# A spectral transform and MLP on one core: MLP chunks of 512 tokens instead of 470

## The chip, the cores and the metric

The kernel runs on one core of one Trainium2 chip. The metric is device time in microseconds of one execution. Before the change three runs gave 2720.18, 2721.32 and 2723.31 us, a median of 2721.32 us.

TensorE (PE) multiplies matrices into the eight PSUM banks; VectorE (DVE), ScalarE (ACT) and GpSimd (POOL) do the elementwise work; SyncE (SP) issues most of the DMAs and ACT some. Each engine runs its instructions in the order in which they were put on its queue.

## The reference

Two stages. First a filter in the frequency domain on x of shape (8, 3008, 256): a real FFT along the sequence, a complex projection of the 256 channels, a soft threshold, and the inverse FFT. Then an MLP on the 24064 tokens that result, with d_model 256 and d_ff 2048.

```python
X = np.fft.rfft(x, axis=1)
Yr = Xr @ w_r - Xi @ w_i + b_r
Yi = Xr @ w_i + Xi @ w_r + b_i
Yr = np.sign(Yr) * np.maximum(np.abs(Yr) - 0.01, 0.0)      # Yi alike
y = np.fft.irfft(Yr + 1j * Yi, n=3008, axis=1)
h = y.reshape(24064, 256) @ w_in
out = np.maximum(0.01 * h, h) @ w_out
```

## The kernel before

The FFT of length 3008 = 47 x 64 is one transform over n1 (47 values, taken as 24 sums and differences) and one over n2 (64 values). The 64 values of n2 are written as 13 g + s, with five g and thirteen s; s = 12 has only four g that carry data. The stages for one batch are these generators and functions.

- `fwd(b)` (line 169): loads x in seven pieces (`load`), makes sums and differences (`fold`), multiplies by the matrices `fa` (`stage_a`) and stores to `u_dram`.
- `mid(b)` (line 231): for twelve pairs of k1, loads from `u_dram`, transforms over n2 (`stage_b`), projects and thresholds (`proj`), transforms back over k2 (`stage_g`) and stores to `v_dram`.
- `v_load(ci)` and `inverse(ci, eh)` (lines 349, 362): load one (batch, s) pair of sets, that is two neighbours in the list of all (batch, s), and make its tokens: four matmuls for each of the two halves of the channels, then on ACT a copy `odd`, on DVE a sum and a difference into `y`, and the split of `y` into `yh` and `yl`. `odd` and `y` have one buffer each.
- `moe_h(ci, f)` and `moe_o(ci, f)` (lines 389, 407): one of 16 blocks of 128 of the hidden dimension of one chunk of tokens. `moe_h` runs six matmuls into a `psh` bank (two banks), applies leaky relu and splits the result into `gh` and `gl`. `moe_o` runs six matmuls that add to the two `pso` banks of the chunk.

Most operands are held as two parts (`hi` and `lo`, of type float32r), and a product is three matmuls, hi x hi, hi x lo and lo x hi (`products`, line 70). Plain float32 products, used in the prologue and for the two 128-wide transforms, appear as two instructions in the profile.

Tokens come in chunks: one chunk is one pair of sets, 10 x 47 = 470 tokens, or 9 x 47 = 423 where the pair has an s = 12 (matmuls then take 424 columns). There are 44 chunks of 470 and 8 of 423. `moe()` (line 431) goes over chunks and blocks; `moe_o` follows `moe_h` by LAG = 3 steps; at block 4 it loads the next chunk's pair, at blocks 10 and 12 it runs the inverse for it.

The order of the work around it: a prologue does `fwd` of batches 0 to 2, `mid(0)`, and the conversion of the MLP's weights from float64 (`load_mlp`). Then `v_load(0)` and both halves of `inverse(0)` stand ahead of the first `moe_h`. During the MLP of batch b the streams `mid(b + 1)` and `fwd(b + 3)` are put between its steps; the position goes from b to b + 1, and each stream is complete at 0.75 of it. The program is put on the queues by a scheduler that moves instructions ahead where it finds them ready, so the trace doesn't follow the source order to the letter.

Buffers that the change touches: `yh` and `yl` have two each, and two of batch 0's x pieces (`XT`, line 167) and the weights `w_r` and `w_d` (line 97) use the same ones in the prologue.

Of the kernel before, what the change touches and what calls it, by code (L numbers as in the profile page):

```python
# [8 lines left out]
F32 = mybir.dt.float32  # L9
# [15 lines left out]
# High words of float64 numbers, read as float32: the last that float32 holds, and the one that becomes zero.  # L25
# [5 lines left out]
def spectral_mlp_kernel(  # L31
# [38 lines left out]
    def products(dst, pairs):  # L70
        """dst = sum of lhsT.T @ rhs over pairs of operands, each float32 or two parts of it."""
        terms = []
        for l, r in pairs:
            terms += [(l[0], r[0]), (l[0], r[1]), (l[1], r[0])] if len(l) == 2 else [(l[0], r[0])]
        for i, (a, b) in enumerate(terms):
            nc.tensor.matmul(dst, a, b, start=(i == 0), stop=(i == len(terms) - 1))  # L76
# [62 lines left out]
    def load_mlp():  # L139
        """Piece by piece; the last ones stay off the buffers that the MLP needs."""  # L140
# [26 lines left out]
    XT = [(("xa", 3), ("xb", 3))] * 3 + [(("yh", 2), ("gh", LAG + 1)), (("yl", 2), ("gh", LAG + 1))] * 2  # L167
# [63 lines left out]
    def mid(b):  # L231
# [17 lines left out]
        def stage_b(j):  # L249
            """Xr, s Xi and their sum for two k1, with the sign s of the half spectrum."""  # L250
# [26 lines left out]
        def proj(j):  # L277
            """With K = (Xr + Xi) w_r: Yr = K - Xi (w_r + w_i) + b_r, Yi = K + Xr (w_i - w_r) + b_i."""
# [63 lines left out]

# [6 lines left out]
    def v_load(ci):  # L349
        vin = sb.tile([PA, 2, 2, D], F32, name="vin", tag="vin")  # L350
        (b, s, _), (b1, _, _) = chunks[ci]
        for c in range(2):
# [4 lines left out]
            for i, (b_, s_, _) in enumerate(chunks[ci]):  # L357
                vv = v_dram[b_].rearrange("c k (g s) d -> c (k g) s d", g=NG)
                sync.dma_start(vin[:, c, i, :], vv[c, :, s_, :])
        v_t[ci] = vin  # L360

    def inverse(ci, eh):
        """The even and the odd part of the tokens in n1, of which n1 is the sum and 47 - n1 the difference."""
        (_, _, n0), (_, _, n1) = chunks[ci]
        m = n0 + n1
        ne, n = m * NK1, m * N1
        vin = v_t[ci]
# [10 lines left out]
        y = sb.tile([P, NT], F32, name="y", tag="y", bufs=1)  # L378
# [4 lines left out]
        if n % 2:  # L383
            dve.memset(y[:, n:n + 1], 0.0)
            n += 1
        act.copy(yh[:, eh, :n], y[:, :n])
# [231 lines left out]
```

## Time and profile before

| | |
|---|---|
| median of the runs | 2721.32 us |
| profiled execution, span from first to last instruction | 2717.4 us |
| prologue, to the first MLP matmul | 164.0 us |
| from there to the end of the last matmul | 2549.4 us |
| last output copies and stores | 4.0 us |
| granted TensorE clock, mean | 0.994 |
| matmul instructions | 13810, of them 9984 in the MLP |

The profiled execution has no time of its own beside the span; the runs' median is 3.9 us above it. A row of a group reads: source line, engine, operation, output<-inputs, shapes, xcount | busy time in us, mean duration in ns | idle time of the engine before these instructions, and what ended it. A row of the timeline reads: start in us, duration in us, engine, line, operation, and in brackets the idle time before it. A row that begins with two times is a stretch: its length, then for PE, the weight loads, DVE, ACT and POOL the busy time and the number of instructions, then the granted clock, the busy share of the DMA engines and GB/s.

### The profile page before, as it was taken

How to read it: one execution, taken by the hardware profiler on the slowest of the kernel's cores; microseconds unless marked ns; L12 is line 12 of the kernel's file. 1: busy time of each engine (PE TensorE's matmuls, PEld its weight loads, DVE VectorE, ACT ScalarE, POOL GpSimd, SP SyncE). 2: the span in 40 equal slices, each digit the busy share in tenths (PEclk: the TensorE clock that was granted, in tenths of full speed). 3: DMA queues.
4: the chain of work that ended last, by engine and by line, in shares of the span. 5: the costliest groups of instructions: out<-in, count | busy, mean ns of one | idle time of the engine just before them, and what ended most of it. 6: DMA issues, size and time to landing. Idle time of an engine off the chain costs nothing.

```text
span 2717.4 us, 37211 instructions
## 1 busy us (share of the span) xinstructions
PE 2662.3 (98%) x13810; PEld 2376.7 (87%) x13810; DVE 1818.5 (67%) x3236; ACT 1407.4 (52%) x2779; POOL 317.1 (12%) x245
## 2 busy tenths in 40 slices
PE   6789999999999999999999999999999999999999
PEld 3568888988899888998889888999989999899888
DVE  5988776766767676766667766566656666555554
ACT  3455555555555555555555555555545555445454
POOL 3761110111110111110010100000000000000000
PEclk9899999999999999999999999999999999999999
DMA  8642222221221212221221211211111111100000
GB/s 265 193 146 79 70 57 67 63 58 54 59 62 56 60 56 56 78 59 49 64 60 54 65 53 38 63 36 46 41 46 42 38 34 30 41 30 14 15 15 14
DMA packets 122347, 164.79 MB, mean 61 GB/s; under 512 B 13757, under 2 KB 83381, under 8 KB 122165
## 3 DMA queue, kind: packets, MB, share of 16 engines
q1 hardware_dynamic: 78885, 111.27, 13.4%
q10 hardware_dynamic: 43280, 51.14, 7.1%
q8 instruction: 109, 1.79, 0.3%
q14 instruction: 73, 0.60, 0.1%
HBM read 86.59 MB, written 75.76 MB: 60 GB/s over the span
## 4 chain that ended last, share of the span: by engine, by line
PE 92%; DVE 4%; DMA 2%; issue 1%; ACT 1%; SPq 0%; POOL 0%; ACTq 0%; DVEq 0%
PE pso L420 38%; PE psh L76 38%; PE psf L76 10%; PE psf L373 3%; PE psf L258 3%; DVE t L301 1%; DMA u_dram<-xin 1%; DMA xin<-x_dram 0%; DVE t L303 0%; DMA raw<-w_out_dram 0%; DVE cva L129 0%; DVE cva L131 0%; DMA u<-u_dram 0%; DVE cva L130 0%; DVE raw L132 0%
## 5 line engine op out<-in xcount | busy, mean ns | idle before, releaser
L402 DVE TENSOR_TENSOR gf<-gf,psh 128x470 f32<-128x470 f32 (+1 forms) x832 | 529.3, 636 | 416.6 <-ACT gf L401 408.9
L404 DVE TENSOR_TENSOR gl<-gf,gh 128x470 fp32r<-128x470 f32 (+1 forms) x832 | 562.8, 677 | 355.0 <-ACT gh L403 344.7
L401 ACT ACTIVATE gf<-psh 128x470 f32<-128x470 f32 (+1 forms) x832 | 463.5, 557 | 583.8 <-PE psh L76 572.5
L403 ACT CAST gh<-gf 128x470 fp32r<-128x470 f32 (+1 forms) x832 | 482.4, 580 | 469.5 <-DVE gf L402 466.8
L76 PE MATMUL psh<-yh,win_hi 128*128 128x470 f32 (+1 forms) x1664 | 638.1, 383 | 1.2 <-DVE gf L402 0.9
L420 PE MATMUL pso<-gh,wout_lo 128*128 128x470 f32 (+1 forms) x1664 | 619.8, 372 | 0.0
L76 PE MATMUL psh<-yh,win_lo 128*128 128x470 f32 (+1 forms) x1664 | 619.4, 372 | 0.0
L76 PE MATMUL psh<-yl,win_hi 128*128 128x470 f32 (+1 forms) x1664 | 619.0, 372 | 0.1
L420 PE MATMUL pso<-gh,wout_hi 128*128 128x470 f32 (+1 forms) x1664 | 618.1, 372 | 0.0
L420 PE MATMUL pso<-gl,wout_hi 128*128 128x470 f32 (+1 forms) x1664 | 578.8, 375 | 0.0
L76 PEld LDWEIGHTS psh<-yh,win_lo 128*128 128x128 f32 x1664 | 313.4, 188 | 37.2
L420 PEld LDWEIGHTS pso<-gh,wout_lo 128*128 128x128 f32 x1664 | 312.7, 188 | 36.7
L420 PEld LDWEIGHTS pso<-gh,wout_hi 128*128 128x128 f32 x1664 | 313.1, 188 | 34.5
L76 PEld LDWEIGHTS psh<-yh,win_hi 128*128 128x128 f32 x1664 | 314.0, 189 | 33.4 <-DVE gf L402 2.9
L76 PEld LDWEIGHTS psh<-yl,win_hi 128*128 128x128 f32 x1664 | 316.1, 190 | 29.1 <-DVE yl L387 0.4
L420 PEld LDWEIGHTS pso<-gl,wout_hi 128*128 128x128 f32 x1664 | 308.9, 188 | 33.1 <-DVE gl L404 0.2
L293 POOL TENSOR_TENSOR kb<-bias,kc 128x512 f32<-128x512 f32 x84 | 113.0, 1345 | 1482.8 <-ACT kc L292 1318.3
L301 DVE TENSOR_TENSOR t<-psf,kb 64x256 f32<-64x256 f32 x384 | 161.8, 421 | 30.5 <-PE psf L76 26.2
L373 PEld LDWEIGHTS psf<-ga,vin 120*128 120x128 f32 x832 | 119.8, 191 | 10.1 <-DMA vin<-v_dram 2.2
L373 PE MATMUL psf<-ga,vin 120*128 120x128 f32 x832 | 123.4, 274 | 1.2 <-DMA vin<-v_dram 1.2
L189 POOL TENSOR_TENSOR xs<-xin,xin 120x512 f32<-120x512 f32 (+1 forms) x49 | 64.9, 1325 | 472.3 <-DMA xin<-x_dram 218.1
L258 PEld LDWEIGHTS psf<-fb,u 128*128 128x128 f32 x672 | 96.2, 191 | 13.9 <-ACT kc L292 3.5
(110 smaller groups left out, 2610.1 us busy)
## 6 DMA issues: line engine op xcount, KB each, us to landing
u<-u_dram SPq DMA_DIRECT2D x192, 128.0 KB, 2.8
v_dram<-v ACTq DMA_DIRECT2D x192, 128.0 KB, 2.5
xin<-x_dram SPq DMA_DIRECT2D x96, 240.0 KB, 3.1
u_dram<-xin ACTq DMA_DIRECT2D x96, 240.0 KB, 2.4
vin<-v_dram SPq DMA_DIRECT2D x96, 240.0 KB, 3.3
out_dram<-ob SPq DMA_DIRECT2D x88, 235.0 KB, 2.3
raw<-w_in_dram SPq DMA_DIRECT2D x8, 512.0 KB, 5.6
raw<-w_out_dram SPq DMA_DIRECT2D x8, 512.0 KB, 4.8
```

Of the source, the lines that this page charges most:

```text
L76: nc.tensor.matmul(dst, a, b, start=(i == 0), stop=(i == len(terms) - 1))
L189: eng.tensor_add(xs, xa, xb)
L258: nc.tensor.matmul(pv[:, dh, :, i, :], u[:, i, s], fbt[:, 0:k + 2:k + 1, :], start=True, stop=True)
L293: pool.tensor_add(kb, bias, kc.unsqueeze(1).broadcast_to([P, 2, D]))
L301: dve.tensor_add(t[64 * r:64 * (r + 1), i, :], ps_y[s, r * D:(r + 1) * D], kb[s, r, :])
L373: nc.tensor.matmul(py[:, o:o + P], vin[:, c, i, s], consts["ga"][:, c, :], start=True, stop=True)
L401: act.mul(gf[:, :n], ph[:, :n], SLOPE)
L402: dve.tensor_max(gf[:, :n], gf[:, :n], ph[:, :n])
L403: act.copy(gh[:, :n], gf[:, :n])
L404: dve.tensor_sub(gl[:, :n], gf[:, :n], gh[:, :n].bitcast(F32))
L420: nc.tensor.matmul(po[:, :n], a[:, f, s], r[:, :n], start=(f == 0 and j == 0), stop=(f == NF - 1 and j == 2),)
```

## The change

- The MLP's chunks no longer follow the pairs. The 24064 tokens are cut into 47 chunks of 512. A pair's inverse writes its columns into the one or two chunks that they fall into, so ACT's and DVE's split of `y` becomes two pieces where a chunk border lies in the pair. `yh` and `yl` get a third buffer.
- A pair is loaded and inverted one chunk ahead of the chunk in which its first token lies: `v_load` at block 3, the inverse at blocks 9 and 10; where a chunk has two such pairs, the second at block 5 and at blocks 12 and 13.
- Ahead of the first MLP step stand the pairs that begin in chunk 0: pairs 0 and 1.
- The streams `mid(b + 1)` and `fwd(b + 3)` run from one reading position to the next and are complete at 0.95 of the way. `read[b]` is block 3 of the chunk before the one in which the first pair with data of batch b begins.
- Leaky relu: one ACT instruction (Prelu with alpha 0.01) from `psh` to `gf` replaces an ACT multiplication and a DVE maximum.
- The odd column of 423-token chunks, and its memset, are gone.
- The reserved SBUF scratch for dynamic DMAs is set to 1024 bytes.

```diff
-    NT = 2 * NG * N1
+    NT = 512
+    NV = 2 * NG * N1
+    READ = 3
...
-        r = sb.tile([P, NH, D], F32, name="w_r", tag="yh")
-        d = sb.tile([P, NH, D], F32, name="w_d", tag="yl")
+        r = sb.tile([P, NH, D], F32, name="w_r", tag="yh", bufs=3)
+        d = sb.tile([P, NH, D], F32, name="w_d", tag="yl", bufs=3)
...
-    XT = [(("xa", 3), ("xb", 3))] * 3 + [(("yh", 2), ("gh", LAG + 1)), (("yl", 2), ("gh", LAG + 1))] * 2
+    XT = [(("xa", 3), ("xb", 3))] * 3 + [(("yh", 3), ("gh", LAG + 1)), (("yl", 3), ("gh", LAG + 1))] * 2
...
-    chunks = _chunks(NB)
-    nch = len(chunks)
-    t0 = [sum(N1 * sum(n for _, _, n in c) for c in chunks[:i]) for i in range(nch + 1)]
+    pairs = _pairs(NB)
+    p0 = [sum(N1 * sum(n for _, _, n in c) for c in pairs[:i]) for i in range(len(pairs) + 1)]
+    nch = p0[-1] // NT
...
-        if eh == 0:
-            y_t[ci] = tuple(sb.tile([P, NH, NT], F32R, name=n_, tag=n_) for n_ in ("yh", "yl"))
-        yh, yl = y_t[ci]
...
-        act.copy(yh[:, eh, :n], y[:, :n])
-        dve.tensor_sub(yl[:, eh, :n], y[:, :n], yh[:, eh, :n].bitcast(F32))
+        lo = p0[pi]
+        while lo < p0[pi + 1]:
+            ci = lo // NT
+            hi = min((ci + 1) * NT, p0[pi + 1])
+            if ci not in y_t:
+                y_t[ci] = tuple(sb.tile([P, NH, NT], F32R, name=n_, tag=n_, bufs=3) for n_ in ("yh", "yl"))
+            yh, yl = (t[:, eh, lo - ci * NT:hi - ci * NT] for t in y_t[ci])
+            yp = y[:, lo - p0[pi]:hi - p0[pi]]
+            act.copy(yh, yp)
+            dve.tensor_sub(yl, yp, yh.bitcast(F32))
+            lo = hi
...
-        act.mul(gf[:, :n], ph[:, :n], SLOPE)
-        dve.tensor_max(gf[:, :n], gf[:, :n], ph[:, :n])
+        act.activation(gf[:, :n], ph[:, :n], AF.Prelu, alpha=SLOPE)
...
+    due = [[p for p in range(len(pairs)) if p0[p] // NT == ci] for ci in range(nch)]
+    read = [
+        max(0, min(p0[p] // NT for p, c in enumerate(pairs) if any(x[0] == b for x in c)) - 1) + READ / NF
+        for b in range(NB)
+    ]
...
             if ci + 1 < nch:
-                if f == 4:
-                    v_load(ci + 1)
-                if f in (10, 12):
-                    inverse(ci + 1, (f - 10) // 2)
-            yield 2 * (ci + (f + 1) / NF) / NS
+                for k, p in enumerate(due[ci + 1]):
+                    if f == READ + 2 * k:
+                        v_load(p)
+                    if f in (READ + 6 + 3 * k, READ + 7 + 3 * k):
+                        inverse(p, f - READ - 6 - 3 * k)
+            yield ci + (f + 1) / NF
...
-    v_load(0)
-    inverse(0, 0)
-    inverse(0, 1)
-    m, fw, cur = None, None, -1
+    for p in due[0]:
+        v_load(p)
+    for p in due[0]:
+        for h in range(2):
+            inverse(p, h)
+    cur, streams = -1, ()
     for pos in moe():
-        b = min(int(pos), NB - 1)
-        if b > cur:
-            cur = b
-            for s in (m, fw):
-                if s:
-                    s.finish()
-            m = mids[b] if b + 1 < NB else None
-            fw = Stream(fwd(b + NPRE), FWD) if b + NPRE < NB else None
-        frac = pos - b
-        if m:
-            m.to(frac / 0.75)
-        if fw:
-            fw.to(frac / 0.75)
+        while cur + 1 < NB - 1 and pos >= (read[cur + 1] if cur >= 0 else 0):
+            for s in streams:
+                s.finish()
+            cur += 1
+            streams = [mids[cur]] + ([Stream(fwd(cur + NPRE), FWD)] if cur + NPRE < NB else [])
+        frac = (pos - read[cur]) / (read[cur + 1] - read[cur]) if cur + 1 < NB else 1
+        for s in streams:
+            s.to(frac / 0.95)
...
-    nc = bacc.Bacc("TRN2", target_bir_lowering=False, num_devices=1)
+    nc = bacc.Bacc("TRN2", target_bir_lowering=False, num_devices=1, dynamic_dma_scratch_size=1024)
```

More of the change, by code (lines that the diff above doesn't have):

```diff
@@ L341, in mid, with v_load @@
                 yield 3 * CS
-    chunks = _chunks(NB)
-    nch = len(chunks)
-    t0 = [sum(N1 * sum(n for _, _, n in c) for c in chunks[:i]) for i in range(nch + 1)]
+    pairs = _pairs(NB)
+    p0 = [sum(N1 * sum(n for _, _, n in c) for c in pairs[:i]) for i in range(len(pairs) + 1)]
+    nch = p0[-1] // NT
     y_t, v_t, g_t, o_t = {}, {}, {}, {}
-    def v_load(ci):
+    def v_load(pi):
         vin = sb.tile([PA, 2, 2, D], F32, name="vin", tag="vin")
-        (b, s, _), (b1, _, _) = chunks[ci]
+        (b, s, _), (b1, _, _) = pairs[pi]
         for c in range(2):
@@ L356, in v_load, with inverse @@
                 continue
-            for i, (b_, s_, _) in enumerate(chunks[ci]):
+            for i, (b_, s_, _) in enumerate(pairs[pi]):
                 vv = v_dram[b_].rearrange("c k (g s) d -> c (k g) s d", g=NG)
                 sync.dma_start(vin[:, c, i, :], vv[c, :, s_, :])
-        v_t[ci] = vin
-    def inverse(ci, eh):
-        (_, _, n0), (_, _, n1) = chunks[ci]
+        v_t[pi] = vin
+    def inverse(pi, eh):
+        (_, _, n0), (_, _, n1) = pairs[pi]
         m = n0 + n1
         ne, n = m * NK1, m * N1
-        vin = v_t[ci]
+        vin = v_t[pi]
         py = bank("psf", 3)
@@ L581, in _tokens @@
     cols = []
-    for c in _chunks(nb):
+    for c in _pairs(nb):
         n2 = [(b, NS * g + s) for b, s, n in c for g in range(n)]
```

17 lines of the change are left out of this document (6 added, 11 removed).

## The prediction

> **What bounds the kernel now.** I read the page first: engine shares, the chain that ended last, and the four instructions that each MLP step runs off TensorE.
>
> ```profile
> span 2717.4 us, 37211 instructions
> PE 2662.3 (98%) x13810; PEld 2376.7 (87%) x13810; DVE 1818.5 (67%) x3236; ACT 1407.4 (52%) x2779; POOL 317.1 (12%) x245
> PE 92%; DVE 4%; DMA 2%; issue 1%; ACT 1%; SPq 0%; POOL 0%; ACTq 0%; DVEq 0%
> ...
> L402 DVE TENSOR_TENSOR gf<-gf,psh 128x470 f32<-128x470 f32 (+1 forms) x832 | 529.3, 636 | 416.6 <-ACT gf L401 408.9
> L404 DVE TENSOR_TENSOR gl<-gf,gh 128x470 fp32r<-128x470 f32 (+1 forms) x832 | 562.8, 677 | 355.0 <-ACT gh L403 344.7
> L401 ACT ACTIVATE gf<-psh 128x470 f32<-128x470 f32 (+1 forms) x832 | 463.5, 557 | 583.8 <-PE psh L76 572.5
> L403 ACT CAST gh<-gf 128x470 fp32r<-128x470 f32 (+1 forms) x832 | 482.4, 580 | 469.5 <-DVE gf L402 466.8
> ```
>
> TensorE is the chain. Second view: busy time by stretch. The columns are PE, weight loads, DVE, ACT, POOL; an x counts the instructions that touch the stretch. The first row runs from the first MLP matmul to the last matmul's end; the last two hold MLP matmuls alone, of 470 and of 424 columns.
>
> ```profile
> 164.02:2713.40 2549.38, 2547.24 (x13404) 2306.02 (x13404) 1690.27 (x3050) 1329.98 (x2627) 223.18 (x171) 1.00 0.17 50
> 2560.00:2670.00 110.00, 110.00 (x517) 96.95 (x516) 59.26 (x98) 53.11 (x96) 0.00 (x0) 1.00 0.03 9
> 2680.00:2710.00 30.00, 30.00 (x158) 29.21 (x157) 15.72 (x27) 14.03 (x27) 0.00 (x0) 1.00 0.05 18
> ```
>
> Third: TensorE's groups by shape. Busy PE time overlaps itself (a matmul's duration includes its way through the array), so I need the spacing of starts.
>
> ```profile
> L76 PE MATMUL psh<-yh,win_lo 128*128 128x470 f32 x1408 | 528.7, 376 | 0.0
> L420 PE MATMUL pso<-gh,wout_hi 128*128 128x470 f32 x1408 | 527.3, 375 | 0.0
> L373 PE MATMUL psf<-ga,vin 120*128 120x128 f32 x832 | 123.4, 274 | 1.2 <-DMA vin<-v_dram 1.2
> L76 PE MATMUL psh<-yh,win_lo 128*128 128x424 f32 x256 | 90.6, 354 | 0.0
> L76 PE MATMUL psf<-wd_lo,eh 128*128 128x256 f32 x168 | 47.2, 281 | 0.0
> L76 PE MATMUL psf<-zl,gb_hi 128*128 128x512 f32 x84 | 33.4, 397 | 0.0
> L76 PE MATMUL psf<-zh,gb_lo 128*128 128x512 f32 x84 | 33.0, 393 | 0.0
> L76 PE MATMUL psf<-xl,fa_hi 120*120 120x512 f32 x60 | 23.7, 396 | 0.3 <-DVE xl L199 0.3
> ```
>
> Of the 517 that touch 110 us, 375/213 = 1.8 began earlier, so 515.2 begin inside: one every 213.5 ns at 470 columns. Likewise 158 - 1.8 in 30 us: 192.1 ns at 424. Duration less spacing is 162 ns in both shapes (375.5 - 213.5, 354 - 192.1), so I read the other spacings as duration less 162: 119 at 256 columns, 112 for each of the two passes of a plain float32 matmul of 128, about 232 at 512.
>
> Check of the whole: MLP 8448 x 213.5 + 1536 x 192.1 = 1803.6 + 295.1 = 2098.7 us; inverse 816 x 112 = 91 (this and the next counts without those before 164 us); transform over n2 about 648 x 112 = 73; projection 1494 x 119 = 178; its 512-wide and the forward ones 432 x 232 = 100; 30 of 256 = 4. Together 2545 of the 2549.4 us between first MLP matmul and last. Waits of TensorE in the MLP part are thus worth a few us at most, and no gain can come from a wait there.
>
> **The change part by part.**
>
> *Chunks of 512.* Matmul columns hardly change: 192 x (44 x 470 + 8 x 424) = 192 x 24072 before, 192 x 24064 after, in 47 x 192 = 9024 matmuls for 9984. So only a cost per matmul can be saved, and it is small: from 424 to 470 columns the spacing rises 21.4 ns for 46 columns, 0.465 each, and 424 x 0.465 is already more than 192.1. All hangs on the 512 spacing, which no MLP matmul shows but the transforms do:
>
> ```profile
> 1002.34 0.40 PE L76 MATMUL psf<-zh,gb_hi 128*128 128x512 f32 x1
> 1002.58 0.39 PE L76 MATMUL psf<-zl,gb_hi 128*128 128x512 f32 x1
> 1002.80 0.39 PE L76 MATMUL psf<-zh,gb_lo 128*128 128x512 f32 x1
> 1003.03 0.61 PE L373 MATMUL psf<-ga,vin 120*128 120x128 f32 x4
> ```
>
> Here 0.69 us for three, 230.0 each: the low end. Durations of 393 to 397 say 231 to 235; the line through 424 and 470 says 213.5 + 42 x 0.465 = 233.0: the high end. I take 231.8: nearest to the 393 row (231), and a little over it for the 397 beside it. After: 9024 x 231.8 = 2091.8, that is -7 us (230.0 gives -23, 233.0 gives +4).
>
> The Trainium skill (TensorE: Matmul & The Clock Gate, section Back-to-back issue gap) gives columns / 2.4 + 2.5 ns. By it 470 columns take 198.3 and 512 take 215.8, and the edit would save 3.0 us in place of 7. The trace does not agree: 213.5 at 470.
>
> *Leaky relu in one instruction.* 832 DVE maxima (636 ns) go; ACT keeps two instructions a step. From the rows, a Prelu of 512 columns costs between 0.56 and 1.2 us (mul and max together); I take 0.60, for it has the form of the multiply it replaces. ACT then needs 0.6 + 0.62 in a step of 12 x 231.8 = 2.78 us, DVE one subtraction of 0.74. A psh bank is written again one and a half steps, 4.2 us, after its last write, so even 1.2 us is covered. No wait of TensorE on these exists to be won:
>
> ```profile
> PE psf L76 <- DVE t L301: 0.8, 1, 0.8
> PE psf L76 <- DVE xl L199: 0.3, 1, 0.3
> PE psh L76 <- DVE gf L402: 0.2, 1, 0.2
> ```
>
> These are all its waits after 200 us. The gain is 0; if ACT's cover were gone, the next late thing would be gh for moe_o, three steps later.
>
> *Spread to 0.95 and earlier reading.* The same transforms lie under the same matmuls: 0. DMA counts are those of before but for 94 output stores in place of 104. SP has nothing else moved past it than v_load, one step earlier and by pair. A batch's transforms now end some 0.3 chunks before its v_load, that is 1.1 chunks or some 55 us before the chunk that reads it (a chunk lasts 2549/47 = 54 us). From v store to yl takes 2.5 + 3.3 us for the two DMAs and 6.6 for an inverse (below): 12.4. A cover of 40 us is left; without it each of seven borders would cost what is missing.
>
> ```profile
> v_dram<-v ACTq DMA_DIRECT2D x192, 128.0 KB, 2.5
> ...
> vin<-v_dram SPq DMA_DIRECT2D x96, 240.0 KB, 3.3
> ```
>
> *The start.* Chunk 0 now needs pairs 0 and 1, so two more inverses stand ahead of the first MLP matmul.
>
> ```profile
> 155.87 1.60 PE L373 MATMUL psf<-ga,vin 120*128 120x128 f32 x12 [1.23 <-DMA vin<-v_dram]
> 163.05 0.66 PE L76 MATMUL psh<-xin,fa 120*120 120x256 f32 x2 [3.16 <-ACT xin L208]
> 164.02 0.76 PE L76 MATMUL psh<-yh,win_hi 128*128 128x470 f32 x1 [0.31 <-ACT xin L208]
> ...
> 156.62 0.36 ACT L379 COPY odd<-psf 128x240 f32<-128x240 f32 x1 [2.42 <-PE psf L373]
> 162.61 0.64 DVE L387 TENSOR_TENSOR yl<-y,yh 128x470 fp32r<-128x470 f32 x1
> ```
>
> Pair 0 takes 156.62 to 163.25, 6.6 us, through single buffers odd and y, with moe_h(0, 0) queued on TensorE behind it. The second pair adds at most 6.6; at least 2.9, since chunk 0 takes only 42 of its columns (two times odd 0.36, sum and difference 0.8, small pieces 0.3). I take 5. Its 16 inverse matmuls (16 x 112 = 1.8 us) run in that gap and leave the stream: net +3 (+1 to +5). Splitting 46 inverses at chunk borders adds small ACT and DVE pieces, covered as above.
>
> *Third buffers of yh and yl.* w_r need no longer wait for a yh buffer; SP issued it late, and DVE sat on it:
>
> ```profile
> 29.86 0.40 SPq L104 DMA_DIRECT2D w_r<-w_r_dram  x1
> ...
> 34.95 1.37 DVE L95 TENSOR_TENSOR wr_lo<-w_r,wr_hi 128x512 fp32r<-128x512 f32 x1 [10.94 <-ACT wr_hi L94]
> ...
> 40.09 1.13 PE L258 MATMUL pso<-fb,u 128*128 128x128 f32 x8 [1.23 <-DMA u<-u_dram]
> 41.06 1.03 PE L76 MATMUL psf<-w_r,ef 128*128 128x256 f32 x4
> ```
>
> Its first reader on TensorE did not wait for it, but for u. So 0, with at most 10.9 to be won.
>
> Sum against the profiled span: 2717.4 - 7 + 3 = 2713.4. The runs' median lies 3.9 above that span, so **2717.5 us**, about 0.15% below before.
>
> **The rivals.**
> 1. Faster: a cost per matmul. If 512 columns take 230.0, as in the triplet, 2717.4 - 23 + 3 + 3.9 = 2701; 231.0 gives 2710. For it: the triplet; against: the 393 to 397 rows and the 424 and 470 line. Chance 0.26.
> 2. Faster: the start-up. The w_r wait turns out to have held the chain: 2717.5 - 10.9 = 2707. Against: the u wait. Chance 0.08.
> 3. Slower: the price per column grows with length. It is (192.1 - 119) / 168 = 0.435 from 256 to 424 columns and 0.465 to 470; at 0.49 beyond, 512 take 234.1 in every MLP matmul: 9024 x 234.1 = 2112.5, +14, so 2738. It decides from 232.9 on, where the loss passes 0.2%. For it: those slopes; against: the 393 and 396 rows. Chance 0.13.
> 4. Slower: a border between batches is late after all, in case the in-order queues hold a batch's last v store back by more than the 40 us; 10 us beyond it at seven borders would give 2788. Chance 0.04.
> 5. Prelu does not come at the price of a multiply but with a table change. The trace has one load, 1283 ns:
>
> ```profile
> L94 ACT ACT_TABLE_LOAD x1 | 1.3, 1283 | 1.9 <-POOL zero L236 1.9
> ```
>
> Two loads a step beside 1.2 us are 3.8 us in a step of 2.78: 752 x 1.0 = 750 us more, 3470. For it nothing but that Prelu is new here. Chance 0.02. The Trainium skill (ScalarE: Activation LUTs, section Table sets: the hidden batching unit) has cheap functions in every set, with relu, copy and abs as examples; no run here shows Prelu.
>
> **How the numbers follow.** The forecast, 2717.5, has 0.47, with its own range of 2713 to 2726. A change under 0.2% (5.4 us) is about what cannot be told from none. Faster by more, below 2715.9: rivals 1 and 2, 0.34. Slower by more, above 2726.8: rivals 3 to 5, 0.19. The range runs from 2702, the 230.0 ns end, to 2736, nearly the 234 ns end; rivals 4 and 5 and the tails, under 0.2, lie outside.
>
> **What would show it.** The MLP matmuls' mean duration at 512 columns should be 393 to 395 ns; 392 or less is rival 1, 396 or more rival 3. The first MLP matmul should start near 169 us (164 + 5) and the last should end 2541 us later (2549.4 - 7 - 1.8). ACT's Prelu should last about 0.60 us, with one table load in all, and TensorE's waits after 200 us should stay near 1 us; a wait on yl or vin in them is rival 4. The w_r copy should come early and move nothing on TensorE. The prediction is wrong if time comes or goes where TensorE was already dense for another reason than the matmul spacing.

## The result, and the profile after

The changed kernel takes 2726.07 us (median of 20 runs, 2722.74 to 2727.83) against 2720.41 for the kernel before (20 runs, 2718.28 to 2723.68): a ratio of 1.0018, 95% interval [1.0012, 1.0025]. It is slower, by 5.7 us; 2717.5 had been forecast. The profiled execution has a span of 2724.9 us, 7.5 more than before's.

The page of the kernel after first: span, busy time, the chain, the three instructions left to an MLP step off TensorE, and three groups of MLP matmuls.

```profile
span 2724.9 us, 34405 instructions
...
PE 2668.1 (98%) x12850; PEld 2200.8 (81%) x12850; DVE 1316.2 (48%) x2400; ACT 1408.0 (52%) x2701; POOL 314.7 (12%) x245
...
PE 94%; DVE 3%; DMA 2%; issue 1%; ACT 1%; SPq 0%; POOL 0%; ACTq 0%; DVEq 0%
...
L409 DVE TENSOR_TENSOR gl<-gf,gh 128x512 fp32r<-128x512 f32 x752 | 531.5, 707 | 1193.8 <-ACT gh L408 1179.1
L407 ACT ACTIVATE gf<-psh 128x512 f32<-128x512 f32 x752 | 449.7, 598 | 901.2 <-PE psh L79 875.8
L79 PE MATMUL psh<-yh,win_hi 128*128 128x512 f32 x1504 | 605.4, 403 | 4.9 <-ACT yh L392 4.4
L424 PE MATMUL pso<-gh,wout_hi 128*128 128x512 f32 x1504 | 596.6, 397 | 0.0
L79 PE MATMUL psh<-yl,win_hi 128*128 128x512 f32 x1504 | 594.0, 395 | 0.9 <-DVE yl L393 0.9
...
L408 ACT CAST gh<-gf 128x512 fp32r<-128x512 f32 x752 | 466.8, 621 | 21.1 <-ACT gf L407 0.5
```

DVE lost 502 us of work and ACT kept its own; TensorE is the chain as before, so none of that shows in the time. Now busy time by stretch, for the kernel after: from the third MLP step to the last matmul's end, and a stretch of MLP matmuls alone.

```profile
181.05:2720.90 2539.85, 2539.85 (x12416) 2122.10 (x12416) 1181.33 (x2197) 1326.11 (x2538) 211.39 (x164) 1.00 0.17 49
...
2560.00:2670.00 110.00, 110.00 (x475) 89.19 (x474) 30.93 (x50) 52.17 (x91) 0.00 (x0) 1.00 0.03 10
```

The same stretch of the kernel before, which begins with its third MLP step:

```profile
168.50:2713.60 2545.10, 2543.09 (x13392) 2302.62 (x13392) 1686.23 (x3044) 1328.75 (x2625) 220.53 (x169) 1.00 0.17 49
```

So the dense part got shorter, by 2545.1 - 2539.9 = 5.2 us, and the loss is all ahead of it: the third MLP step begins at 181.05 us where it began at 168.5, 12.5 later. 12.5 - 5.2 is 7.3 of the 7.5 us between the two spans. The second row gives the spacing: 475 less the 397/232 = 1.7 that began earlier is 473.3 in 110 us, 232.4 ns for 512 columns.

The start, in TensorE's timeline of the kernel after:

```profile
160.92 2.04 PE L377 MATMUL psf<-ga,vin 120*128 120x128 f32 x8 [1.38 <-DMA vin<-v_dram]
...
168.03 1.13 PE L377 MATMUL psf<-ga,vin 120*128 120x128 f32 x8 [0.22 <-DVE y L383]
173.52 1.22 PE L79 MATMUL psh<-yh,win_hi 128*128 128x512 f32 x2 [4.35 <-ACT yh L392]
174.54 0.63 PE L79 MATMUL psh<-yl,win_hi 128*128 128x512 f32 x1
174.97 0.63 PE L79 MATMUL psh<-yh,win_lo 128*128 128x512 f32 x1
...
178.44 0.80 PE L79 MATMUL psh<-yl,win_hi 128*128 128x512 f32 x1 [0.93 <-DVE yl L393]
...
181.05 0.79 PE L79 MATMUL psh<-yh,win_hi 128*128 128x512 f32 x1 [0.53 <-ACT gf L407]
```

Three things are to be seen. The first inverse matmul comes at 160.9, 7.0 us later than before's, whose first four stand in this row of its timeline:

```profile
153.93 0.71 PE L373 MATMUL psf<-ga,vin 120*128 120x128 f32 x4
```

The first MLP matmul waits 4.35 us for yh, at 173.5 instead of the 164.0 of before. And then the matmuls come every 0.43 us, half as fast as later. The clock says why: busy time by stretch of 10 us, after.

```profile
160.00:170.00 10.00, 8.02 (x38) 6.39 (x38) 7.04 (x16) 5.36 (x12) 5.49 (x6) 0.72 0.85 259
170.00:180.00 10.00, 5.55 (x12) 3.50 (x12) 8.10 (x15) 3.83 (x10) 6.43 (x5) 0.62 0.74 213
180.00:190.00 10.00, 9.47 (x31) 7.14 (x30) 5.57 (x9) 7.01 (x12) 4.83 (x4) 0.70 0.16 54
```

And the same three stretches of the kernel before:

```profile
160.00:170.00 10.00, 6.48 (x21) 5.01 (x22) 9.00 (x16) 5.95 (x13) 5.43 (x4) 0.83 0.90 254
170.00:180.00 10.00, 10.00 (x48) 8.53 (x47) 7.66 (x12) 5.60 (x11) 7.00 (x6) 1.00 0.16 56
180.00:190.00 10.00, 10.00 (x48) 8.67 (x47) 7.74 (x13) 5.93 (x11) 4.66 (x4) 1.00 0.15 52
```

The third number from the right is the granted clock. After, it is 0.72, 0.62 and 0.70, so 10 x (0.28 + 0.38 + 0.30) = 9.6 us of clock are missing in these 30; before, 1.7. TensorE was busy for 23 of the 30 us, so not all of that is lost time. The trace puts the clock at half from 172.4 to 186.0 us after, and from 163.9 to 167.3 before. In these stretches run some 23 MLP matmuls after (0.43 us each in place of 0.23) and 8 before (0.39 in place of 0.21), so the slow clock costs about 3 us more than before, as an estimate from these spacings. Gaps in TensorE's stream at the start are paid twice here: as waits, and as a slow clock after them. The Trainium skill (TensorE: Matmul & The Clock Gate, section What's actually happening) says that the gate falls to half after an idle window of about 3.4 us and is released by a busy one. The trace agrees in that the clock falls to half at 172.4, inside the wait of 4.35 us that ends at 173.5; it comes back at 186.0, after two more waits of 0.93 and 0.53 us.

Two things kept yh late. The first is that the inverse's input is late. The last copy of batch 0's `v` on ACT and the load of `vin` on SP, before:

```profile
147.29 0.59 ACT L324 COPY v<-pso 128x512 f32<-128x512 f32 x1 [0.33 <-issue]
150.79 1.69 SPq L355 DMA_DIRECT2D vin<-v_dram  x4
```

And after:

```profile
151.00 0.59 ACT L327 COPY v<-pso 128x512 f32<-128x512 f32 x1 [0.49 <-DMA xin<-x_dram]
155.02 1.76 SPq L358 DMA_DIRECT2D vin<-v_dram  x4
```

The copy is 3.7 us later and the load 4.2, and its first part lands 5.8 us after its issue where it took 3.1. The second is ACT's own order, in the timeline of the kernel after:

```profile
161.45 0.57 ACT L211 COPY xin<-psh 120x512 f32<-120x512 f32 x1
...
164.71 0.59 ACT L211 COPY xin<-psh 120x512 f32<-120x512 f32 x1 [2.69 <-PE psh L79]
...
166.00 0.36 ACT L211 COPY xin<-psh 120x256 f32<-120x256 f32 x1
166.25 0.63 ACT L138 CAST wout_hi<-cva 128x512 fp32r<-128x512 f32 x1
166.78 0.37 ACT L380 COPY odd<-psf 128x240 f32<-128x240 f32 x1
...
173.24 0.85 ACT L392 CAST yh<-y 128x42 fp32r<-128x42 f32 x2 [1.68 <-DVE y L381]
```

The first eight of the inverse's matmuls run from 160.9 to 163.0, but ACT copies odd only at 166.8, 3.8 us after them: ahead of it in its queue stand the last copies of the forward transform and a conversion of w_out. Before, ACT stood idle when it came to odd, at 156.6. And from the first odd to the last yh of the second pair's first half go another 7 us.

### The profile page after: what moved, and what is told of

Its sections match the earlier page's. It is cut to its first block, busy times and chain, and to the rows that moved or that the text cites. A ratio compares the mean times of both kernels' runs of the same rounds, so it can differ in the third digit from the quotient of the medians.

```text
span 2724.9 us, 34405 instructions
## 1 busy us (share of the span) xinstructions
PE 2668.1 (98%) x12850; PEld 2200.8 (81%) x12850; DVE 1316.2 (48%) x2400; ACT 1408.0 (52%) x2701; POOL 314.7 (12%) x245
## 4 chain that ended last, share of the span: by engine, by line
PE 94%; DVE 3%; DMA 2%; issue 1%; ACT 1%; SPq 0%; POOL 0%; ACTq 0%; DVEq 0%
PE pso L424 39%; PE psh L79 38%; PE psf L79 10%; PE psf L377 3%; PE psf L261 3%; DMA xin<-x_dram 1%; DVE c L305 0%; DVE t L304 0%; DMA u_dram<-xin 0%; DVE t L306 0%; DMA u<-u_dram 0%; DMA raw<-w_in_dram 0%; DVE cva L132 0%; DMA fb<-fb_dram 0%; DVE cva L134 0%
## 5 line engine op out<-in xcount | busy, mean ns | idle before, releaser
L409 DVE TENSOR_TENSOR gl<-gf,gh 128x512 fp32r<-128x512 f32 x752 | 531.5, 707 | 1193.8 <-ACT gh L408 1179.1
L407 ACT ACTIVATE gf<-psh 128x512 f32<-128x512 f32 x752 | 449.7, 598 | 901.2 <-PE psh L79 875.8
L79 PE MATMUL psh<-yh,win_hi 128*128 128x512 f32 x1504 | 605.4, 403 | 4.9 <-ACT yh L392 4.4
L424 PE MATMUL pso<-gh,wout_hi 128*128 128x512 f32 x1504 | 596.6, 397 | 0.0
L79 PE MATMUL psh<-yh,win_lo 128*128 128x512 f32 x1504 | 595.0, 396 | 0.0
L79 PE MATMUL psh<-yl,win_hi 128*128 128x512 f32 x1504 | 594.0, 395 | 0.9 <-DVE yl L393 0.9
L424 PE MATMUL pso<-gh,wout_lo 128*128 128x512 f32 x1504 | 593.4, 395 | 0.0
L424 PE MATMUL pso<-gl,wout_hi 128*128 128x512 f32 x1504 | 580.6, 395 | 0.0
L408 ACT CAST gh<-gf 128x512 fp32r<-128x512 f32 x752 | 466.8, 621 | 21.1 <-ACT gf L407 0.5
L393 DVE TENSOR_TENSOR yl<-y,yh 128x470 fp32r<-128x470 f32 (+46 forms) x196 | 90.6, 487 | 38.3 <-ACT yh L392 36.3
```

What stands on the lines that cost most here:

```text
L393: dve.tensor_sub(yl, yp, yh.bitcast(F32))
L407: act.activation(gf[:, :n], ph[:, :n], AF.Prelu, alpha=SLOPE)
L408: act.copy(gh[:, :n], gf[:, :n])
L409: dve.tensor_sub(gl[:, :n], gf[:, :n], gh[:, :n].bitcast(F32))
L424: nc.tensor.matmul(po[:, :n], a[:, f, s], r[:, :n], start=(f == 0 and j == 0), stop=(f == NF - 1 and j == 2),)
```

## The experiments

Times are medians; each ratio is against runs of the kernel before on the same chip. Spacings are the mean over unbroken runs of twelve MLP matmuls of one length in the trace, between 300 and 2700 us.

**Prelu alone**, on the old chunks.

```diff
-        act.mul(gf[:, :n], ph[:, :n], SLOPE)
-        dve.tensor_max(gf[:, :n], gf[:, :n], ph[:, :n])
+        act.activation(gf[:, :n], ph[:, :n], AF.Prelu, alpha=SLOPE)
```

> The kernel before with the one ACT instruction for leaky relu alone. Theory S: DVE loses some 530 us of work and nothing else moves: the median within 2 us of before, TensorE's stretch from the third MLP step on unchanged. Rival D (relief of DVE is worth time, in the prologue or by waits hidden in the dense part): 2716 or less.

2721.14 us, ratio 1.0001 [0.9992, 1.0010]. The group row of that kernel, on its page:

```profile
L401 ACT ACTIVATE gf<-psh 128x470 f32<-128x470 f32 (+1 forms) x832 | 464.8, 559 | 850.6 <-PE psh L76 798.0
```

559 ns, against 557 for the multiply before. The exchange costs and gains nothing that shows, within the interval of some 2.5 us: the removed maximum was covered.

**Third buffers alone**, on the old chunks: yh and yl with three buffers, w_r and w_d in one of them each, and the smaller DMA scratch.

```diff
-        r = sb.tile([P, NH, D], F32, name="w_r", tag="yh")
-        d = sb.tile([P, NH, D], F32, name="w_d", tag="yl")
+        r = sb.tile([P, NH, D], F32, name="w_r", tag="yh", bufs=3)
+        d = sb.tile([P, NH, D], F32, name="w_d", tag="yl", bufs=3)
...
```

> The kernel before with the third buffers of yh and yl (prologue uses included) and the smaller scratch alone. Theory S in its first form (all of the loss is the second pair): third MLP step at 168 to 169 us as before, no change. Rival P: w_r and w_d load earlier, the prologue falls into another order, the last copy of mid(0) moves from 147.3 towards 151 us as in the changed kernel, and the median is 3 to 5 us above before.

2734.74 us, ratio 1.0054 [1.0042, 1.0067]. What the prediction put at 0 costs 14 us here. The third MLP step comes at 176.1 instead of 168.5, and the dense part, with the same number of matmuls as before's row above, is 8.8 us longer:

```profile
176.10:2730.00 2553.90, 2552.26 (x13392) 2306.25 (x13392) 1689.17 (x3044) 1331.93 (x2624) 213.99 (x166) 1.00 0.17 49
```

The spacing at 470 columns is 214.4 ns (before: 213.4), and 8448 x 1.0 = 8.4 us is nearly that. Two runs take this apart. **The scratch alone**:

```diff
-    nc = bacc.Bacc("TRN2", target_bir_lowering=False, num_devices=1)
+    nc = bacc.Bacc("TRN2", target_bir_lowering=False, num_devices=1, dynamic_dma_scratch_size=1024)
```

> The kernel before with the DMA scratch of 1024 alone: every engine keeps its instructions in their order, only the addresses of buffers can move. In the run with third buffers and this scratch the MLP matmuls of 470 columns came every 214.4 ns, before every 213.4 (dense part 2553.9 us against 2545.1). Theory, the scratch moved the buffers and that sets the spacing: 214.4 ns here too, 8448 x 1.0 = 8.4 us more, about 2729 us. Rival, the third buffers themselves (or the new order in the prologue) did it: 213.4 ns, 2720 to 2721 us, no change.

2721.51 us, ratio 1.0002 [0.9993, 1.0010], spacing 213.4 ns: the scratch does nothing. Its third MLP step came at 171.2, 2.7 later than before's with the same order on every engine; a start in one profiled execution can't be trusted to better than that, and a later pair of kernels shows 3.5. **Third buffers, but w_r and w_d in buffers of gh**, where w_r waits again for x piece 3:

```diff
-        r = sb.tile([P, NH, D], F32, name="w_r", tag="yh", bufs=3)
-        d = sb.tile([P, NH, D], F32, name="w_d", tag="yl", bufs=3)
+        r = sb.tile([P, NH, D], F32, name="w_r", tag="gh", bufs=LAG + 1)
+        d = sb.tile([P, NH, D], F32, name="w_d", tag="gh", bufs=LAG + 1)
```

> The kernel before with third buffers of yh and yl (2734.7 us when w_r took one of them), and w_r and w_d in buffers of gh, so that w_r waits as before. Theory, the early w_r costs the start and the third buffers' places cost the spacing: the third MLP step back from 176 to about 169 to 171 us, the 470 spacing still 214.4 ns (+8.4 us), so about 2729 us. Rival 1, the spacing came with the other order too: 213.4 ns, 2721 us. Rival 2, the early w_r costs nothing on the old chunks: 2734.7 us again.

2730.60 us, ratio 1.0033 [1.0021, 1.0045]. The third MLP step is back at 170.7 and the spacing stays at 214.3. So the two losses are separate: the third buffer of w_r and w_d cost the start, about 0.2% on these chunks (1.0054 and 1.0033, with intervals that just overlap), and the third buffers of yh and yl themselves cost the spacing of 470 columns. Whether they cost 512 columns something too was not run: no kernel here has chunks of 512 with two buffers of yh and yl, and 1 ns of spacing would be 9 us there.

**w_r held in the changed kernel.** A first try asked for w_r to be issued after the store of x piece 3, and put three quarters of batch 0's forward transform ahead of the loads of the weights:

```diff
+        with tc.issue_after(third[0].ins):
+            sync.dma_start(r, w_r.rearrange("(a p) f -> p a f", p=P))
...
+    f0.to(0.75)
```

> The kernel after with the load of w_r held until x piece 3 is stored, as the shared buffer held it before. Theory, the early w_r load is what changed the prologue: the last v copy of batch 0 comes near 147.3 us in place of 151.0, the first MLP matmul near 170 in place of 173.5, and the time is some 3.6 us less, 2722 us. Rival, the third buffers for x pieces, or nothing of w_r, did it: last v copy near 151, 2726 us.

2725.26 us, ratio 1.0015 [1.0006, 1.0024], no different from the kernel after. It tells nothing about w_r, for the load still went out early. The store that it was to follow is issued by ACT and the load by SP, and the order was not held. The row in SP's queue of that kernel:

```profile
16.28 0.38 SPq L107 DMA_DIRECT2D w_r<-w_r_dram  x1
```

Then through the buffer, as in the run before:

```diff
-        r = sb.tile([P, NH, D], F32, name="w_r", tag="yh", bufs=3)
-        d = sb.tile([P, NH, D], F32, name="w_d", tag="yl", bufs=3)
+        r = sb.tile([P, NH, D], F32, name="w_r", tag="gh", bufs=LAG + 1)
+        d = sb.tile([P, NH, D], F32, name="w_d", tag="gh", bufs=LAG + 1)
```

> The kernel after with w_r and w_d in buffers of gh (four of them, which x pieces 3 to 6 fill first), so that w_r waits for the store of x piece 3 as it did before; in the run meant to hold w_r by an order of issue it still went out at 16.3 us. Theory, the early w_r is what let the MLP weight conversions run ahead of batch 0: w_r issued near 30 us, last v copy of batch 0 near 147 to 148 us in place of 151, first MLP matmul near 170, time some 3 us less, 2723 us. Rival, what moved the copies is something else (third buffers for yh and yl as such): last v copy near 151, time 2726 us.

2718.09 us, ratio 0.9993 [0.9984, 1.0002]. Against the 1.0018 of the kernel after that is 0.25%, 6.8 us, twice what was expected, and the changed kernel is no longer slower than before. The load, in SP's queue of this kernel:

```profile
29.28 0.59 SPq L107 DMA_DIRECT2D w_r<-w_r_dram  x1
```

The last copy of the forward transform and the first one of odd, in ACT's timeline of the same kernel:

```profile
154.60 0.67 ACT L211 COPY xin<-psh 120x256 f32<-120x256 f32 x2
...
161.09 0.36 ACT L380 COPY odd<-psf 128x240 f32<-128x240 f32 x1 [2.80 <-PE psf L377]
```

And the start of the MLP, in TensorE's timeline:

```profile
158.74 6.31 PE L377 MATMUL psf<-ga,vin 120*128 120x128 f32 x32 [4.34 <-DMA vin<-v_dram]
170.58 1.22 PE L79 MATMUL psh<-yh,win_hi 128*128 128x512 f32 x2 [5.53 <-ACT yh L392]
...
174.16 0.39 PE L79 MATMUL psh<-yl,win_hi 128*128 128x512 f32 x1
174.39 0.40 PE L79 MATMUL psh<-yh,win_lo 128*128 128x512 f32 x1
...
175.48 0.50 PE L79 MATMUL psh<-yh,win_hi 128*128 128x512 f32 x1 [0.22 <-ACT gf L407]
```

With w_r at 29.3 us the last copies of the forward transform stand at 154.6 on ACT, and odd follows its matmuls at 161.1; with w_r at 15.9 these copies ran to 167.8 and odd came at 166.8. The wait for yh is even longer (5.53 us), but it ends 3 us earlier, the matmuls are at full speed within the second step (0.23 us apart at 174.16), and the third step begins at 175.5. The inverse itself starts only 2.2 us earlier, and the last copy of v came at 149.8, not at 147 to 148 as expected; so most of what moved is ACT's copy of odd, 5.7 us. The rows show that the order of the prologue differs; the order is fixed when the kernel is built, and why it answers so strongly to where w_r stands was not looked into. It is not simply before's order either: there the last of these copies stood at 163.6. The edit moves w_d and w_r together out of the buffers of yl and yh, and no run holds the load late by itself, so that the load time is the cause, and not the buffers shared, is argued. What speaks for it is all the traces together: in the nine kernels of this case that issue w_r at 15.9 to 17.6 us ACT's first copy of odd stands at 163.2 to 167.5, in the eight that issue it at 29.3 to 30.4 it stands at 156.6 to 162.1.

**One pair ahead of the first MLP matmul**: 48 chunks, the first of 470, which pair 0 fills, and 47 of 502.

```diff
-    nch = p0[-1] // NT
+    sizes = [470] + [502] * 47
+    nch = len(sizes)
+    c0 = [sum(sizes[:i]) for i in range(nch + 1)]
...
```

> The changed kernel with one edit: 48 chunks, the first of 470 tokens (pair 0 alone) and 47 of 502, so that only pair 0 stands ahead of the first MLP matmul. Columns are the same. Theory S (the start: the second pair ahead of the first matmul, with the clock that falls meanwhile, costs the changed kernel about 8 us, and the dense part is neutral): the third MLP step starts at 172 to 175 us in place of 181.0, and the median is 2717 to 2720. Rival P (the prologue was put in another order, and the second pair only fills a gap): the third step stays at 179 or later, 2724 to 2727. Rival C (512 columns are dear): 502 columns are cheaper per column, the stretch from the third step to the last matmul shrinks by 5 us or more.

2713.98 us, ratio 0.9977 [0.9968, 0.9986], 12.1 less than the kernel after and less than before. More of it is length than start: 502 columns come every 226.8 ns, so 192 x (47 x 226.8 + 213.4) = 2087.6 stands against 9024 x 232.4 = 2097.2, 9.6 us; the second pair is left with 2.5, a difference that is no larger than the interval of the two medians. The trace of this kernel seems to say otherwise, for its third step comes 6.2 us earlier (174.8) and its dense part is only 3.1 shorter. But the dense part now holds the second pair's inverse matmuls (1.8), 3.3 us of idle time and a stretch of half clock near 207 us, and the profiled execution, 2717.75 us, is the slowest of its eleven.

**Two buffers each for odd and y** in the kernel after.

```diff
-        odd = sb.tile([P, 2 * NG * NK1], F32, name="odd", tag="odd", bufs=1)[:, :ne]
-        y = sb.tile([P, NV], F32, name="y", tag="y", bufs=1)
+        odd = sb.tile([P, 2 * NG * NK1], F32, name="odd", tag="odd", bufs=2)[:, :ne]
+        y = sb.tile([P, NV], F32, name="y", tag="y", bufs=2)
```

> The changed kernel with two buffers each for odd and y. Theory S with the single buffers as the reason for the long chain: the four halves overlap, the third MLP step starts 2 to 4 us earlier than 181.0, median 2722 to 2724. If the chain is set by the order of other work on ACT and DVE instead: no change, 2725 to 2727.

2721.21 us, ratio 1.0005 [0.9997, 1.0014], some 4 us gained. Up to the first copy of odd every engine keeps the order of the kernel after; still that copy came at 163.2 in place of 166.8, which is the spread of one execution. From it to the third step go 10.7 us in place of 14.3: these 3.6 are the edit's. Its longest waits of TensorE between 145 and 215 us show the link that got shorter (1.5 us for yh, where the first MLP matmul of the kernel after waited 4.35):

```profile
PE psh L79 <- POOL xin L193: 2.9, 1, 2.9
PE psh L79 <- ACT yh L392: 1.5, 1, 1.5
PE psf L377 <- DMA vin<-v_dram: 1.5, 1, 1.5
PE psh L79 <- DVE yl L393: 1.4, 1, 1.4
```

**Both repairs at once**, w_r in gh and two buffers, on the chunks of 512:

```diff
-        r = sb.tile([P, NH, D], F32, name="w_r", tag="yh", bufs=3)
+        r = sb.tile([P, NH, D], F32, name="w_r", tag="gh", bufs=LAG + 1)
...
-        odd = sb.tile([P, 2 * NG * NK1], F32, name="odd", tag="odd", bufs=1)[:, :ne]
+        odd = sb.tile([P, 2 * NG * NK1], F32, name="odd", tag="odd", bufs=2)[:, :ne]
...
```

> The kernel after with both repairs of the start: two buffers each for odd and y, and w_r and w_d in buffers of gh; chunks of 512 and two pairs ahead of the first MLP matmul stay. Alone they gave 2721.2 and 2718.1 us. Theory, the whole loss lies in the start and the two causes are separate: the third MLP step begins near 170 us, the time is 2726 less 5 less 7, about 2714 us, and the rest of the run as in the kernel after (dense part 2538 to 2540 us). Rival, both repairs shorten the same stretch, in which the conversions of w_out crowd ACT and DVE: 2718 us, as w_r alone.

2718.55 us, ratio 0.9989 [0.9981, 0.9998]. The rival holds on these chunks: with w_r held, the two buffers give nothing that shows. Here they are two ways to the same few microseconds, not two losses.

**The price of 512 columns.** First the same order of instructions at other addresses: the tiles of yh, yl, gh and gl 536 wide.

```diff
-                y_t[ci] = tuple(sb.tile([P, NH, NT], F32R, name=n_, tag=n_, bufs=3) for n_ in ("yh", "yl"))
+                y_t[ci] = tuple(sb.tile([P, NH, NT + 24], F32R, name=n_, tag=n_, bufs=3) for n_ in ("yh", "yl"))
...
```

> The kernel after, with the tiles of yh, yl, gh and gl 536 wide, of which 512 are used: the order of every engine is unchanged, only addresses and the distance of rows move. Theory, placement sets the spacing in part: the 512 spacing leaves 232.4 ns by half a nanosecond or more (on the line from 470 at 213.4 to 502 at 226.8 it would be 231.0, that is 9024 x 1.4 = 12.6 us less, 2713 us). Rival, the length alone sets it: 232.4 ns and 2726 us, the time of the kernel after.

2726.92 us, ratio 1.0019 [1.0010, 1.0027], spacing 232.5 ns (232.4): nothing changed. Then many lengths in one kernel:

```diff
+    sizes = [470] + [n for n in (512, 500, 508, 490, 504, 510, 496, 506, 488) for _ in range(5)] + [512, 512]
...
```

> The kernel after with 48 chunks of many sizes: 470, then five each of 512, 500, 508, 490, 504, 510, 496, 506 and 488, then two of 512; every engine does the same otherwise. It measures the MLP matmul's spacing at each length in one run. Theory, a smooth line: 0.42 to 0.46 ns per column between 470 (213.4) and 512 (232.4), so 488 near 221.6, 496 near 225.2, 504 near 228.8, 508 near 230.6. Rival, steps by alignment: 496, 504 and 512 (multiples of 8) or 512 alone lie 1 ns or more off the line through 470 and 502 (0.42 per column: 488 at 220.9, 496 at 224.3, 504 at 227.6, 510 at 230.1). Time by the line 2713 to 2718 us.

2724.31 us, ratio 1.0015 [1.0005, 1.0025]; 2713 to 2718 had been expected. The spacings, with those of the other kernels:

```
columns  424    470    490    496    500    502    504    506    508    510    512
ns       192.1  213.4  223.3  225.0  226.8  226.8  231.9  228.2  229.0  231.8  232.4
per col  0.4531 0.4540 0.4557 0.4536 0.4536 0.4518 0.4601 0.4510 0.4508 0.4545 0.4539
```

The ninth length, 488, has 220.0 ns, 0.4508 per column. In the run of many lengths a value moves by up to 1 ns with the rows that are averaged. There is no smooth line: 504 columns cost more than 506 or 508. This also says why the time was missed: 192 matmuls a chunk at these spacings sum to 2096.7 us, against 2097.2 with 512 throughout. The groups of the kernel with many sizes, by shape, say so in their durations too:

```profile
L431 PE MATMUL pso<-gh,wout_hi 128*128 128x504 f32 x160 | 63.2, 395 | 0.0
...
L431 PE MATMUL pso<-gh,wout_hi 128*128 128x508 f32 x160 | 62.9, 393 | 0.0
...
L431 PE MATMUL pso<-gh,wout_hi 128*128 128x506 f32 x160 | 62.5, 391 | 0.0
```

The rival of steps by multiples of 8 does not fit either (504 is off, 496 is not). Whether 508 keeps its price in a whole kernel was tried on the repaired kernel below:

```diff
-    sizes = [470] + [502] * 47
+    sizes = [348] + [508] * 46 + [348]
```

> The repaired kernel with one pair ahead of the first MLP matmul (2707.2 us with chunks of 470 and 47 of 502), on chunks of 348, 46 of 508 and 348. Theory, the lengths that the run of many sizes showed hold in a whole kernel: 508 columns at 229.0 ns and 348 near 158 give 192 x (46 x 229.0 + 2 x 158) = 2083 us of MLP matmuls against 2087 with 470 and 502, about 2703 us. Rival, the spacing of 508 is another when all chunks have it (231 on the line from 470 to 512): 192 x (46 x 231 + 2 x 158) = 2101, about 2720 us.

2706.97 us, ratio 0.9945 [0.9932, 0.9959]. The spacing held, 229.0 ns (348 columns take 160.0, not 158), but the time is that of 502 columns within the interval. 192 x (46 x 229.0 + 2 x 160) = 2084.0 would win 3.6 us against 2087.6. In its profile the third MLP step begins at 172.3, against 167.9 with 470 and 502, 4.4 us later, which would take that back; but this execution is the slowest of its five.

**Spread of 0.75** in place of 0.95 in the kernel after.

```diff
-            s.to(frac / 0.95)
+            s.to(frac / 0.75)
```

> The kernel after with the transforms spread over 0.75 of the way to the reading of their result in place of 0.95. Theory, the same work lies under the same dense TensorE: 2726 us, no wait of TensorE on yl or vin after 200 us. Rival, the spread of 0.95 crowds the border between batches, and 0.75 gives back part of the loss: 2722 us or less.

2724.80 us, ratio 1.0013 [1.0004, 1.0022]; it cannot be told from the kernel after. No transform is late at either value: TensorE has no wait after 200 us in either trace.

**The repairs together** on chunks of 470 and 502: first with two buffers for odd and y (the issue order of the first try did not hold w_r here either), then with w_r in gh besides.

```diff
+    sizes = [470] + [502] * 47
...
+        y = sb.tile([P, NV], F32, name="y", tag="y", bufs=2)
...
+        r = sb.tile([P, NH, D], F32, name="w_r", tag="gh", bufs=LAG + 1)
...
```

> The kernel after with a first chunk of 470 and 47 of 502 (one pair ahead of the first MLP matmul), two buffers each for odd and y, and w_r held as before. Theory, the start's losses are separate: from 2714.0 us of the 470 + 502 kernel, less 3.6 for w_r and up to 3 for odd and y, 2708 to 2711 us. Rival, with one pair nothing is left to win and the waits near 201 to 207 us stay: 2714 us.

> The kernel with chunks of 470 and 47 of 502 and two buffers each for odd and y, which took 2710.9 us, with w_r and w_d in buffers of gh besides. Theory (early w_r costs some 3 us in the prologue): 2708 us. Rival (it costs nothing): 2711 us.

2710.91 us, ratio 0.9963 [0.9951, 0.9976], and 2707.17 us, ratio 0.9953 [0.9940, 0.9965]. The second beats both kernels, by 0.5% the one before. Its gain over the first, 3.7 us, goes with w_r's and w_d's buffer; every one of its runs is below every one of the first, but the two intervals overlap. Here the two repairs add up (3.1 and 3.7 us from the kernel with 470 and 502 alone), where on 512 columns they did not; together they give about 7 us in both. Against both repairs on 512 columns (2718.55) it is 11.4 less, of which the columns' 9.6 leave 1.8 for the second pair.

The start and the dense part of these kernels side by side, in us from the profiled executions' traces (ACT's first copy of odd; start of the third MLP step; from there to the end of the last matmul):

```
kernel                            w_r out   first odd   third step   dense part
before                            29.9      156.6       168.5        2545.1
after                             15.9      166.8       181.0        2539.9
after, odd and y twice            16.2      163.2       173.9        2539.7
after, w_r in gh                  29.3      161.1       175.5        2538.2
after, both                       29.5      158.9       172.8        2539.8
470 + 502                         17.6      167.5       174.8        2536.8
470 + 502, odd and y twice        16.9      165.9       172.9        2532.6
470 + 502, both                   29.5      160.4       167.9        2533.1
```

## Why the prediction was wrong

It had forecast 2717.5 us, a change too small to tell, and the time is 2726.07: 8.6 us off, and on the slower side. The measured value lies inside the range of 2702 to 2736, by luck: that range was made from the price of a column, and the loss lies elsewhere. The forecast's own range, 2713 to 2726, ends just below it. Two terms of the sum failed. The column term, -7, was mis-sized, and it alone made the forecast point to faster: with -1.5 the sum is about +1.5. The term of the third buffers, put at 0 with no bound for a loss, is the step that made the kernel slower: taking w_r and w_d out of them gives 6.8 us back and ends the loss.

1. *Chunks of 512, -7 us*: right in kind, wrong in size. The column count is unchanged and the saving hung on the 512 spacing, as said. The spacing is 232.4 where 231.8 was taken, and 9024 x 232.4 = 2097.2 against 2098.7 is -1.5, not -7. (2098.7 was made with 213.5 at 470 columns; with the 213.4 of the experiments it is 2097.9, and the gain is 0.7.) What failed was to choose within the row of transforms: the durations of 393 to 397 gave 231 to 235, and the value was put near the 393, under the pull of one triplet at 230.0. The right value stood in the trace of before: from a 512-wide matmul of the transforms to the next start it is 232 ns, the median of all 429 after 200 us, with a mean of 232.4 when breaks above 300 ns are left out. A line between lengths would have been no safer, for 504 and 506 columns differ by 3.7 ns the wrong way round. The sign by durations misled too: 393 to 395 was forecast and 396 or more was to mean rival 3; the groups read 395 to 397, and 403 for the two with yh and win_hi in each step, 396.8 on average, but the spacing stayed below the 232.9 from which rival 3 was to decide. The Trainium skill's rule for the gap (TensorE: Matmul & The Clock Gate, section Back-to-back issue gap), which it states for a single matmul at full clock, gives 215.8 at 512 and 211.7 at 502, 4.1 apart; the runs show 232.4 and 226.8, 5.6 apart, and steps that no rule linear in the columns has.

2. *Third buffers, 0*: this is the step that made the kernel slower. The prediction looked at w_r's reader on TensorE, found that it waited for u, and took the early load as harmless, with at most 10.9 to be won; the copy was to come early and move nothing on TensorE. It did come early, at 15.9 us. No bound was set for a loss. Held back through another buffer, w_r and w_d give 0.25% on the chunks of 512, 0.21% on the old chunks and 0.10% on 470 and 502: 3 to 7 us, of which only the first is well clear of its interval. What changes with it is the order in which the prologue's work stands on the engines, and in the order that goes with the early load ACT reaches the inverse's copies late. The way from the load to that order stays open.

3. *The start, net +3*: nothing speaks against its own part. The second pair is left with 1.8 to 2.5 us when the columns' 9.6 are taken off the two comparisons above, net of its inverses, which the forecast took off too; this is a difference within the intervals and was not measured by itself. By the traces the third step comes 4.9 and 6.2 us later with the second pair (172.8 against 167.9, 181.0 against 174.8), where the prediction took 5 before the inverses. But the first MLP matmul was to start at 169 and started at 173.5, and the first two steps took 7.5 us, at half clock and with 1.5 us of waits, instead of 4.5. The prediction costed the second pair through odd and y alone. It did not ask when vin would come, what stood ahead of these copies on ACT, nor what a gap does to the clock behind it.

4. *Prelu, 0*: right, in price (0.598 us for 0.60, one table load as before) and in effect (ratio 1.0001 alone).

5. *Spread and earlier reading, 0*: right. No row of TensorE's waits is left after 200 us, and 0.75 gives the same time.

6. *The end 2541 us after the first MLP matmul*: it is 2720.9 - 173.5 = 2547.4, of which the slow first steps are 3. From the third step on, the dense part is 5.2 shorter than before: 1.5 for columns, 1.8 for the inverses moved ahead of it, and 2.0 for idle time, which the two rows of this stretch show (2545.10 - 2543.09, and none after). These make 5.3, but half the clock was still missing until 186 us, which costs the dense part about 2 us, so some 2 us of shortening are not accounted for.

Put together: -1.5 for columns, +2 to +3 for the second pair and +3 to +7 for the buffers of w_r and w_d make +4 to +8; 5.7 was measured. Each of these is a difference of medians with an interval of some 2 to 3 us, so the sum fits but can't be split finer. Rivals 3 to 5 are ruled out as the cause: the price of a column is below 232.9, no border is late, and the table is loaded once. Rival 2 had the right place with the wrong sign. What the third buffers do to the spacing of 512 columns is the term that no run shows.

## What to carry to other kernels

A buffer count is a scheduling edit. Where a new buffer frees an early load, ask not only who waits for the load but what else the freed order lets run ahead, and give the term a bound on the losing side; then test it by taking away the freedom through another buffer. And in a kernel that is dense for 94% of its span, look for the loss of a few microseconds in the prologue, where one gap cost its own length and then a slow clock. And take a price from all the rows of a shape that the trace has, not from one triplet.

## What the runs showed of the hardware

- The spacing of float32r matmuls in these kernels is not linear in the columns: 228.2 ns at 506, 231.9 at 504, 226.8 at both 500 and 502. 0.4508 ns per column at 508 against 0.4539 at 512 is 14 us over this kernel's matmuls.
- It can move by 1 ns with the buffers: 470 columns took 213.4 ns with two buffers of yh and yl and 214.4 with three, twice, under different orders of the prologue. Tiles 24 columns wider did nothing to 512 (232.5). What it depends on stays open.
- The two 42-column subtractions of the start took 0.38 and 1.26 us; the slow one began 0.13 us after a POOL operation of 1.33 us and ended 0.06 after it. It is one case. The two, in DVE's timeline of the kernel after:

```profile
173.50 0.38 DVE L393 TENSOR_TENSOR yl<-y,yh 128x42 fp32r<-128x42 f32 x1
...
177.13 1.26 DVE L393 TENSOR_TENSOR yl<-y,yh 128x42 fp32r<-128x42 f32 x1
```

And the operation in POOL's:

```profile
177.00 1.33 POOL L193 TENSOR_TENSOR xin<-xin,xin 120x512 f32<-120x512 f32 x1
```
